# Gate products moved to GpSimd, the last two packs scored by halves, and 131 instead of 130 packs taken off ScalarE

## The chip, the cores and the metric

The kernel runs on one core of one Trainium2 chip. The metric is the device time of one launch in microseconds (us), as a median over runs; less is better. The engines are called PE (TensorE), ACT (ScalarE), DVE (VectorE), POOL (GpSimd) and SP (SyncE, which here only issues DMAs).

## The reference

There are 2048 tokens of width 512 and 32 heads of 16. Two attention branches read the same `x`; a gate per token mixes them. `x @ wqkv` and the final `@ wo` are there in both.

```python
g = sigmoid((x * gate_w).sum(-1, keepdims=True))
# branch A: softmax attention
scores = einsum("bhqd,bhkd->bhqk", q, k) * (Dh ** -0.5)
o = einsum("bhqk,bhkd->bhqd", softmax(scores), v)        # then @ wo
# branch B: linear attention, its features are two softmaxes over 16 numbers
phi_q = concat([softmax(pq), softmax(-pq)]); phi_k = ...  # pq = q @ w_phi
num = phi_q @ (phi_k^T v); den = phi_q . sum(phi_k)       # then num / den @ wo
out = g * a + (1 - g) * b
```

Branch A has 32 heads x 2048 x 2048 scores, and each wants an exponential. That is most of the work.

## The kernel before

**Units, packs, groups.** A unit is the scores of one head for 128 keys and 512 queries: one matmul with 32 rows of contraction, a tile of 128 x 512 in one bank of PSUM. Four units (four heads, same keys and queries) make a pack; 16 packs (all 2048 keys) make a group, whose sums stand in one PSUM bank; there are 32 groups, so 512 packs. Eight groups go over one chunk of 512 queries, so the run has four chunks.

**Two ways to the exponential.** Most packs go through ACT: `_qk` writes the scores of three or two units into a ring of five PSUM banks (`RING`), and `_exp` (line 1183) reads them in one activation of 1536 or 1024 columns, alternately, into the ring `ET` in SBUF; `_pv` then multiplies them with the values (line 1250). The scores of an activation are written while the activation before it runs. The packs in `self.spot` go another way: `_vector_bits` has DVE turn each score into the bits of a bfloat16 number (line 962, four instructions of 128 x 512 from PSUM for a pack), `_vector_terms` adds a shift to those bits in SBUF for two further terms, and the three terms are all multiplied with the values (12 matmuls for a pack). The first shift is done by DVE for up to two packs together (line 984, 2048 or 4096 columns), and so is the second but for the last of the three `SHIFTS`, which `_pool_term` gives to POOL in two pieces of 1024 columns (line 999). `AWAY` says with one bit mask for each group which packs are in `spot`: key tiles 1, 4, 7, 10 and 13 can be. Its masks have 130 bits set. By chunks of queries these are 29, 34, 32 and 35 packs.

**Normalizing.** When a group is summed, `_norm_a` and `_norm` turn it: DVE transposes the bank into `T1` (line 1271), and after each pair of groups POOL multiplies the sums with the gate (`n_den`, line 1278), DVE takes reciprocals (line 1280) and multiplies the attention values with them into `T2` (`n_mul`, line 1282; 15 of 128 x 512 and one of 128 x 256 for group 30). DMAs on SP's queue turn `T2` into `onTA`, from which the output projection `_out` (its helper `_quarters`, line 651) reads. The last group has a path of its own, `_norm_last` (lines 1105 to 1117), in two halves of 256 queries, all on DVE.

**The end.** `_last_pack` treats pack 511 by halves: all its scores are written, then ACT does the first 256 queries of the four units, then the other 256 (line 1070), and the first half is multiplied with its values and normalized while ACT does the second. The four output tiles of the last chunk follow: two leave PSUM by ACT (line 1619), two by DVE (line 1615), and DMAs store them (line 1624).

**The order.** `Plan.order` is a list scheduler. It gives every engine a fixed queue from costs, priorities and due times; on the chip each engine takes its queue in order and waits on semaphores. `SHIFT` moves the due times of single tasks by up to 14 packs. PE gets matmuls with zeros (line 1257) where it would have little to do. `PORT` and the variable `port` in `order` keep POOL's instructions and certain ones of DVE apart in the plan, and make POOL's wait for DVE's.

Of the kernel before, what the change touches and what calls it, by code (L numbers as in the profile page):

```python
# [389 lines left out]
class _Kernel:  # L390
# [364 lines left out]
    def _gate(self):  # L755
# [44 lines left out]
    AWAY = (26, 27, 26, 31, 22, 13, 15, 15, 31, 15, 13, 31, 30, 23, 31, 15, 29, 31, 26, 27, 31, 26, 31, 21, 31, 31, 28, 31, 31, 11, 23, 31)  # L800

    SHIFT = (
# [166 lines left out]
    def _vector_terms(self, turn, packs):  # L969
# [6 lines left out]
        for k, (shift, scaled) in enumerate(SHIFTS):  # L976
            if k == 2 or k == 1 and turn % self.EVERY == 0:
                for j, pack in enumerate(packs):
                    b = self.b_vp[k][j]
                    self._pool_term(pair, j, k, shift, b, packs[0] + self.TERM)  # L980
                    self.terms[pack].append((lambda k=k, j=j: self.vp[:, k, j], b, scaled))
# [688 lines left out]
```

## Time and profile before

| | |
|---|---|
| time, median of 3 runs | 737.9 us (737.86 to 738.07) |
| the profiled execution, its own time | 737.4 us |
| its span, first to last instruction | 735.6 us |
| ACT busy | 723.5 us, 98% |
| DVE busy | 690.5 us, 94% |
| PE busy, matmuls with zeros included | 713.1 us, 97% |
| POOL busy | 303.8 us, 41% |
| granted PE clock | 1.000 |

Busy time is the union of an engine's instructions. A duration in a row of instructions is longer than the step to the next one on the same engine, since the next starts before the last result is written; where steps matter they are taken from stretches of several instructions. The span is 1.8 us shorter than the time of its execution.

### The profile page before, as it was taken

To read this page: it belongs to the slowest core of one execution; us is meant where nothing else is said; L and a number is where in the kernel's file an instruction comes from. 1 tells how busy PE (TensorE), PEld (TensorE's weight loads), DVE (VectorE), ACT (ScalarE), POOL (GpSimd) and SP (SyncE) were. 2 spreads that over 40 slices of the span, in tenths; PEclk is the share of its full clock that TensorE was granted. 3 is DMA by queue.
4 is the path that set the end of the run, shared out by engine and by line. 5 is a ranking of instruction groups with operands and counts; after the bars stand their busy time and mean duration, and the time that the engine had idled before them with its cause. 6 is when DMAs were issued, how large, how long until landed. Compare 5 with 4: busy or idle time off the path is not lost.

```text
span 735.6 us, 19777 instructions
## 1 busy us (share of the span) xinstructions
PE 713.1 (97%) x8549; PEld 234.4 (32%) x8549; DVE 690.5 (94%) x1085; ACT 723.5 (98%) x636; POOL 303.8 (41%) x318
## 2 busy tenths in 40 slices
PE   8999999999999999999999999999999999999998
PEld 3334233243223223332232233333332233332322
DVE  4899999988999999999999999999999999999996
ACT  6999999999999999999999999999999999999996
POOL 3832342424544424535353344334334444344442
PEclk9999999999999999999999999999999999999999
DMA  9400100001010010100001032042123111003210
GB/s 201 145 10 6 22 2 9 16 4 18 4 15 11 4 20 2 17 11 8 14 2 17 15 61 28 8 83 35 23 45 74 21 16 23 16 25 63 40 29 30
DMA packets 90041, 21.96 MB, mean 30 GB/s; under 512 B 82913, under 2 KB 89441, under 8 KB 89953
## 3 DMA queue, kind: packets, MB, share of 16 engines
q1 hardware_dynamic: 88752, 20.30, 14.5%
q8 instruction: 67, 1.10, 0.7%
q10 hardware_dynamic: 1200, 0.39, 0.2%
q14 instruction: 22, 0.17, 0.1%
HBM read 4.21 MB, written 2.10 MB: 9 GB/s over the span
## 4 chain that ended last, share of the span: by engine, by line
ACT 73%; PE 13%; DVE 11%; DMA 1%; issue 0%; POOL 0%; DVEq 0%; POOLq 0%
ACT ET L1183 70%; PE ps L1131 5%; DVE va L962 4%; PE ps L1250 4%; ACT bq L1425 3%; PE ps L651 2%; DVE vp L984 2%; DVE btree L1414 1%; DMA xT<-in_A_x_dram 1%; PE ps L744 1%; PE ps L1257 1%; DVE bq L1423 0%; DVE VB L1541 0%; DVE nb L1541 0%; DVE rb L1539 0%
## 5 line engine op out<-in xcount | busy, mean ns | idle before, releaser
L1183 ACT ACTIVATE ET<-ps 128x1536 bf16<-128x1536 f32 (+1 forms) x612 | 692.9, 1343 | 4.6 <-PE ps L1131 4.4
L999 POOL TENSOR_SCALAR vp<-va 128x1024 uint16<-128x1024 uint16 x264 | 275.7, 1044 | 337.3 <-DVE vp L984 124.2
L962 DVE TENSOR_SCALAR va<-ps 128x512 uint16<-128x512 f32 x520 | 339.5, 681 | 23.9 <-PE ps L1131 21.7
L1131 PE MATMUL ps<-qT,kT 32*128 32x512 bf16 (+1 forms) x2053 | 311.0, 384 | 10.1 <-ACT ET L1183 5.1
L1131 PEld LDWEIGHTS ps<-qT,kT 32*128 32x128 bf16 x2053 | 82.7, 91 | 258.3 <-ACT ET L1183 146.5
L984 DVE TENSOR_SCALAR vp<-va 128x4096 uint16<-128x4096 uint16 (+1 forms) x151 | 162.0, 1079 | 0.6 <-PE ps L1250 0.2
L1250 PE MATMUL ps<-ET,V 128*32 128x512 bf16 x1532 | 149.0, 385 | 1.3 <-DVE T L1271 1.0
L1250 PE MATMUL ps<-vp,vc 128*32 128x512 bf16 x1040 | 93.9, 384 | 0.3 <-DVE vp L984 0.2
L1250 PEld LDWEIGHTS ps<-ET,V 128*32 128x32 bf16 x1532 | 39.3, 95 | 64.9 <-issue 48.6
L651 PE MATMUL ps<-WB,xT 128*32 128x512 bf16 x768 | 57.4, 382 | 0.5 <-DVE bq L1395 0.3
L1250 PE MATMUL ps<-va,V 128*32 128x512 bf16 x520 | 51.3, 385 | 0.0
L1250 PE MATMUL ps<-vp,V 128*32 128x512 bf16 x520 | 48.2, 383 | 0.3 <-DVE vp L984 0.2
L1257 PE MATMUL ps<-kT,zero 128*32 128x512 bf16 x468 | 42.1, 384 | 0.0
L651 PE MATMUL ps<-xT,WA 128*32 128x512 bf16 x480 | 36.1, 382 | 0.6 <-DVE va L962 0.4
L1250 PEld LDWEIGHTS ps<-vp,vc 128*32 128x32 bf16 x1040 | 24.7, 95 | 35.3 <-issue 20.2
L1425 ACT ACTIVATE bq<-bq 128x2048 bf16<-128x2048 bf16 x16 | 31.5, 1989 | 0.1
L1271 DVE STREAM_TRANSPOSE T<-ps 128x512 f32<-128x512 f32 x31 | 21.9, 708 | 1.1 <-PE ps L1250 1.0
L651 PE MATMUL ps<-WoB,WT 128*32 128x512 bf16 x256 | 22.6, 383 | 0.3 <-DVE va L962 0.3
L1395 DVE CAST bq<-ps 128x512 bf16<-128x512 f32 x32 | 21.7, 678 | 0.3 <-PE ps L651 0.2
L651 PEld LDWEIGHTS ps<-WB,xT 128*32 128x32 bf16 x768 | 15.2, 95 | 19.9 <-issue 10.4
L651 PE MATMUL ps<-WoA,onTA 128*32 128x512 bf16 x256 | 21.2, 381 | 0.0
L744 PE MATMUL ps<-WA,xT 128*128 128x128 bf16 x256 | 19.5, 220 | 0.7 <-DVE va L962 0.4
(94 smaller groups left out, 367.1 us busy)
## 6 DMA issues: line engine op xcount, KB each, us to landing
turned<-T SPq DMA_DIRECT2D x240, 8.0 KB, 1.8
qT<-qs SPq DMA_DIRECT2D x120, 16.0 KB, 1.8
WB<-in_B_wqkv_dram SPq DMA_DIRECT2D x1, 1536.0 KB, 6.9
out_dram<-WB SPq DMA_DIRECT2D x12, 128.0 KB, 2.0
WA<-in_A_wqkv_dram SPq DMA_DIRECT2D x3, 384.0 KB, 5.1
WoA<-in_A_wo_dram SPq DMA_DIRECT2D x1, 512.0 KB, 8.0
WoB<-in_B_wo_dram SPq DMA_DIRECT2D x1, 512.0 KB, 8.9
out_dram<-xT SPq DMA_DIRECT2D x3, 128.0 KB, 1.8
```

Of the source, the lines that this page charges most:

```text
L651: ins = e.matmul(out[32 * g:32 * g + 32], lhs[:, 32 * g:32 * g + 32], rhs, start=start, stop=stop, tile_position=(0, 32 * g), skip_group_c ...
L744: ins = e.matmul(self._bank(job)[:, P * tt:P * tt + P], self.xT[:, c, QCH * j + TOK * tt:QCH * j + TOK * tt + TOK], self.WA[:, 2, c, P * c ...
L962: parts.append(op("DVE", lambda e, j=j, job=job: e.tensor_scalar(self.va[:, pair, side, j, :], self._bank(job), SCALE * LOG2E * 128.0, (12 ...
L984: self.plan.op("DVE", lambda e, k=k, shift=shift: e.tensor_scalar(flat(self.vp[:, k]), flat(self.va[:, pair]), float(shift), None, op0=ALU ...
L999: o = self.plan.op("POOL", lambda e, flat=flat: e.tensor_scalar(flat[0], flat[1], 1.0, float(shift), op0=ALU.mult, op1=ALU.add), 0.08 + n ...
L1131: return e.matmul(out, self.kT[32 * i:32 * i + 32, cp, kt * TOK:(kt + 1) * TOK], self.qT[32 * i:32 * i + 32, s, at], start=True, stop=True ...
L1183: o = plan.op("ACT", lambda e: e.activation(self.ET[:, a % NS:a % NS + n, at], self.ps[:, self._ring(a):self._ring(a) + n, at], ACT.Exp, s ...
L1250: ins = e.matmul(self._bank(ot)[32 * i:32 * i + 32, at], V[:, v0:v0 + 32], tile(), start=(kt == 0), stop=(kt == self.NT - 1), tile_positio ...
L1257: ins = e.matmul(self._bank(ot)[32 * i:32 * i + 32, :], self.zero[:], self.kT[:, 0, 0:QCH], start=False, stop=False, tile_position=(0, 32 ...
L1271: self.turned_out = op("DVE", lambda e: e.transpose(T1[:, side].rearrange("p b s -> p (b s)"), src()), 0.635, deps=last, writes=[b_T1[side ...
L1395: [lambda e, b, k=k: e.tensor_copy(bq[:, k].rearrange("p (g s v) -> p g s v", g=8, s=2)[:, :, 0, :], b.rearrange("p (g v) -> p g v", g=8))],
L1425: op("ACT", lambda e, side=side: e.activation(sides[side], sides[side], ACT.Exp, scale=1.0 - 2 * side), self.c_act(2048) + 0.04, reads=[bu ...
```

## The change

Five things are changed:

1. `AWAY` has 131 bits set instead of 130; by chunks of queries 29, 34, 34 and 34 packs. Other packs of a group are chosen than before.
2. `SHIFT` is another list: of its 756 entries (778 before) six are as they were. So the order of all queues is another.
3. `n_mul` in `_norm` is issued to POOL instead of DVE.
4. Of the last pack in `spot`, the second piece of the last term is done by DVE instead of POOL.
5. `_last_pack` gives way to `_last_packs`: packs 510 and 511 are both taken by halves of the queries. The scores of one unit of pack 510 and one of pack 511, 256 queries each, share one PSUM bank. ACT does the first 256 queries of both packs in two activations of 1024 columns, then the second 256 in one of 1536 and one of 512. The value products of both packs come in two halves as well.

```diff
-    AWAY = (26, 27, 26, 31, 22, 13, 15, 15, 31, 15, 13, 31, 30, 23, 31, 15, 29, 31, 26, 27, 31, 26, 31, 21, 31, 31, 28, 31, 31, 11, 23, 31)
+    AWAY = (18, 31, 14, 27, 27, 26, 29, 27, 31, 15, 13, 31, 29, 15, 31, 27, 21, 31, 31, 15, 14, 23, 31, 31, 14, 31, 29, 31, 29, 27, 27, 31)
     SHIFT = (
...
-    def _pool_term(self, pair, j, k, shift, b, due):
+    def _pool_term(self, pair, j, k, shift, b, due, last):
...
+            if c and last:
+                o = self.plan.op("DVE", lambda e, flat=flat: e.tensor_scalar(
+                    flat[0], flat[1], float(shift), None, op0=ALU.add), 0.07 + n * QCH * 0.00026, reads=[src],
+                    deps=b.readers or b.writers, writes=[sink], name="v_term", prio=due)
+            else:
+                o = self.plan.op("POOL", ...
...
-        cut = len(self.mine) - 4
+        cut = len(self.mine) - 8
...
-        self._last_pack(cut)
+        self._last_packs(cut)
...
+    def _last_packs(self, cut):
...
+        for half in range(2):
+            at, a, of = self._columns(half), 0, {}
+            while a < 4:
+                b = a + 1
+                while b < 4 and self._ring(cut + 4 * half + b) not in (0, 3):
+                    b += 1
+                banks = [self._ring(cut + 4 * half + x) for x in range(a, b)]
+                mine = units[a:b] + units[4 + a:4 + b]
+                m, o = self._halves(mine, banks, cut % NS, a, at, users)
...
+            for p in range(units[0] // 4, self.NPACK):
...
+                o = plan.op("PE", lambda e, p=p, src=src, at=at: self._values(e, self.ot[g], g % 8, p % NT, src, at=at),
+                            0.12, name=f"pv{p}", prio=p + 2.5, kind="col", array=0.1066,
+                            deps=self.b_V[g % 8 // 2][p % NT // 4].writers + [self.pvs[units[0] // 4 - 1]]
+                            + [of[u] for u in range(4 * p, 4 * p + 4)] + ([self.turned_out] if half else []))
...
+            plan.of(f"g{g}", self._norm_last, g, half, done + ([] if half else self.late))
...
+    def _halves(self, units, banks, slot, first, at, users):
+        plan, n = self.plan, len(units)
+        ps = self.ps[:, banks[0]:banks[-1] + 1, :].rearrange("p r (h q) -> p r h q", h=2)
+        to = self.ET[:, slot:slot + 8, at].rearrange("p (k r) q -> p r k q", k=2)[:, first:first + n // 2]
+        def run(e):
+            for k, u in enumerate(units):
+                ins = self._scores(e, u, ps[:, k % (n // 2), k // (n // 2), :], at)
+            return ins
+        m = plan.op("PE", run, 0.23, ..., deps=self.qks[-1:] + [users[r] for r in banks])
...
+        o = plan.op("ACT", lambda e: e.activation(to, ps, ACT.Exp, scale=SCALE), self.c_act(QCH // 2 * n), deps=deps, ...
...
-        op("DVE", lambda e: e.tensor_tensor(
+        op("POOL", lambda e: e.tensor_tensor(
             T2[:].rearrange("p b (s d) -> p s b d", s=2)[:, lo:hi], T1[:, lo:hi, :, 0:16],
-            rinv[:, lo:hi, :, None].to_broadcast([P, n, 16, 16]), ALU.mult), 0.065 + 0.269 * n,
+            rinv[:, lo:hi, :, None].to_broadcast([P, n, 16, 16]), ALU.mult), 0.24 + 0.45 * n,
            reads=reads + [b_rinv], writes=[b_T2], name="n_mul", prio=due)
```

More of the change, by code (lines that the diff above doesn't have):

```diff
@@ L979, in _vector_terms @@
                     b = self.b_vp[k][j]
-                    self._pool_term(pair, j, k, shift, b, packs[0] + self.TERM)
+                    self._pool_term(pair, j, k, shift, b, packs[0] + self.TERM, pack == max(self.spot))
                     self.terms[pack].append((lambda k=k, j=j: self.vp[:, k, j], b, scaled))
@@ L998, in _pool_term @@
             src.writers = bits.writers[c:c + n]
-            o = self.plan.op("POOL", lambda e, flat=flat: e.tensor_scalar(
-                flat[0], flat[1], 1.0, float(shift), op0=ALU.mult, op1=ALU.add), 0.08 + n * QCH * 0.00102,
-                reads=[src], deps=b.readers or b.writers, writes=[sink], name="p_term", prio=due)
+            if c and last:
[3 more added lines that the diff above has]
+            else:
+                o = self.plan.op("POOL", lambda e, flat=flat: e.tensor_scalar(
+                    flat[0], flat[1], 1.0, float(shift), op0=ALU.mult, op1=ALU.add), 0.08 + n * QCH * 0.00102,
+                    reads=[src], deps=b.readers or b.writers, writes=[sink], name="p_term", prio=due)
             bits.readers.append(o)
@@ L1037, in _attention @@
                     self.plan.of(f"y{len(self.pvs)}", self._out, len(self.pvs) // (8 * NT) - 1)
-        self._last_pack(cut)
+        self._last_packs(cut)
         self.plan.of(f"y{len(self.pvs)}", self._out, NQC - 1)
-    def _last_pack(self, cut):
-        plan, NT, NS, p = self.plan, self.NT, self.NSLOT, self.NPACK - 1
-        wrap = cut + -cut % self.RING
-        parts = [(cut, wrap), (wrap, cut + 4)] if cut < wrap < cut + 4 else [(cut, cut + 4)]
-        users = {self._ring(x): self.exps[self.in_group[x]] for x in range(cut - self.RING, cut)}
-        scores = []
-        for a, b in parts:
-            units = self.mine[a:b]
-            def run(e, a=a, units=units):
-                for k, u in enumerate(units):
-                    ins = self._scores(e, u, self.ps[:, self._ring(a + k), :])
-                return ins
-            o = plan.op("PE", run, 0.23, reads=self._score_bufs(units), name=f"qk{len(self.qks)}", prio=-1000, kind="row",
-                        array=0.0533 * (b - a), deps=self.qks[-1:] + [users[self._ring(x)] for x in range(a, b)])
-            o.commit = "now", (units[-1] + 1) // 4
-            o.tiles = [u % 4 for u in units]
-            o.slack = max(0.0, self.exps[-1].cost - self.AHEAD)
-            self.qks.append(o)
-            scores.append(o)
-        g, kt = divmod(p, NT)
-        g8, ot, done = g % 8, self.ot[g], [self.pvs[p - 1]]
-        for hook in self.hooks.get(p, ()):
-            hook()
-        values = []
-        for half in range(2):
-            at, exps = self._columns(half), []
-            for (a, b), m in zip(parts, scores):
-                o = plan.op("ACT", lambda e, a=a, b=b, at=at: e.activation(
-                    self.ET[:, a % NS:a % NS + b - a, at], self.ps[:, self._ring(a):self._ring(a) + b - a, at], ACT.Exp,
-                    scale=SCALE), self.c_act(QCH // 2 * (b - a)),
-                    deps=[m] + [self.pvs[self.mine[x - NS] // 4] for x in (a, b - 1)],
-                    name=f"exp{len(self.exps)}", prio=p + 1)
-                if half:
-                    o.commit = "banks", [self._ring(x) for x in range(a, b)]
-                self.exps.append(o)
-                exps.append(o)
-            src = {u % 4: lambda slot=self.place[u] % NS, at=at: self.ET[:, slot, at] for u in range(4 * p, 4 * p + 4)}
-            plan.tag = f"p{p}"
-            o = plan.op("PE", lambda e, src=src, at=at: self._values(e, ot, g8, kt, src, at=at), 0.12, name=f"pv{p}",
-                        prio=p + 2.5, kind="col", array=0.1066, deps=self.b_V[g8 // 2][kt // 4].writers + done + exps)
-            plan.tag = None
-            o.tiles = list(src)
-            if not half:
-                o.commit = "close", None
-                plan.of(f"g{g}", self._norm_last, g, half, [o] + self.late)
-                done = [o, self.turned_out]
-            else:
-                plan.of(f"g{g}", self._norm_last, g, half, [o])
-        self.pvs.append(o)
-        self.late = []
@@ new lines, in _last_packs @@
+    def _last_packs(self, cut):
+        plan, NT, NS, RING = self.plan, self.NT, self.NSLOT, self.RING
+        users = {}
+        for x in range(cut - RING, cut):
+            users[self._ring(x)] = self.exps[self.in_group[x]]
+        units, packs, left = self.mine[cut:], [], {0: [], 1: []}
+        closing = self.NPACK - 1
+        assert cut % NS <= NS - 8
+        g = closing // NT
+        for half in range(2):
+            at, a, of = self._columns(half), 0, {}
[6 more added lines that the diff above has]
+                m, o = self._halves(mine, banks, cut % NS, a, at, users)
+                if 4 * half + b > 3:
+                    o.commit = "banks", [r for x, r in zip(range(a, b), banks) if 4 * half + x > 2]
+                for r in banks:
+                    users[r] = o
+                for u in mine:
+                    of[u] = o
+                a = b
+            done = []
+            for p in range(units[0] // 4, self.NPACK):
+                if p in self.spot:
+                    if not half:
+                        self._pv(p)
+                    continue
+                if not half:
+                    for hook in self.hooks.get(p, ()):
+                        hook()
+                src = {u % 4: lambda slot=self.place[u] % NS, at=at: self.ET[:, slot, at] for u in range(4 * p, 4 * p + 4)}
+                plan.tag = f"p{p}"
+                o = plan.op("PE", lambda e, p=p, src=src, at=at: self._values(e, self.ot[g], g % 8, p % NT, src, at=at),
+                            0.12, name=f"pv{p}", prio=p + 2.5, kind="col", array=0.1066,
+                            deps=self.b_V[g % 8 // 2][p % NT // 4].writers + [self.pvs[units[0] // 4 - 1]]
+                            + [of[u] for u in range(4 * p, 4 * p + 4)] + ([self.turned_out] if half else []))
+                plan.tag = None
+                o.tiles = [2, 3] if p == closing else [0, 1]
+                if not half and p == closing:
+                    o.commit = "close", None
+                done.append(o)
+                if not half:
+                    self.pvs.append(o)
+            plan.of(f"g{g}", self._norm_last, g, half, done + ([] if half else self.late))
+        self.pvs[-1] = done[-1]
+        self.late = []
@@ new lines, in _halves @@
+    def _halves(self, units, banks, slot, first, at, users):
[6 more added lines that the diff above has]
+            return ins
+        m = plan.op("PE", run, 0.23, reads=self._score_bufs(units), name=f"qk{len(self.qks)}", prio=-1000, kind="row",
+                    array=0.0267 * n, deps=self.qks[-1:] + [users[r] for r in banks])
+        m.commit = "now", (units[-1] + 1) // 4
+        m.tiles = [u % 4 for u in units[:(n + 1) // 2]]
+        m.slack = max(0.0, self.exps[-1].cost - self.AHEAD)
+        self.qks.append(m)
+        deps = [m]
+        if at.start == 0:
+            for u in (units[0], units[-1]):
+                x = self.place[u] - self.NSLOT
+                deps.append(self.pvs[self.mine[x] // 4])
+        o = plan.op("ACT", lambda e: e.activation(to, ps, ACT.Exp, scale=SCALE),
+                    self.c_act(QCH // 2 * n), deps=deps, name=f"exp{len(self.exps)}", prio=units[0] // 4 + 1)
+        self.exps.append(o)
+        return m, o
```

205 rows, old and new, of the table SHIFT are left out of this document.

## The prediction

> **What bounds the kernel now.** I read the page's busy times first, then the waits of ACT, then the chain of work, then DVE's load by stretches, and last the timeline of the end.
>
> ```profile
> PE 713.1 (97%) x8549; PEld 234.4 (32%) x8549; DVE 690.5 (94%) x1085; ACT 723.5 (98%) x636; POOL 303.8 (41%) x318
> ...
> ACT 73%; PE 13%; DVE 11%; DMA 1%; issue 0%; POOL 0%; DVEq 0%; POOLq 0%
> ```
> ```profile
> ACT ET L1183 <- PE ps L1131: 4.4, 1, 4.4
> ACT xT L1619 <- PE ps L651: 2.9, 1, 2.9
> ACT L1183 <- issue: 1.8, 1, 1.8
> ```
>
> The first line ranks the engines; the chain is ACT for 73%. The three lines of waits (us in total, times, longest) are all that ACT ever waited: once before its first activation, once after its last one, and once at launch. So ACT is full from its first exponential to its last, and inside that stretch only less work on ACT can shorten the run. ACT's work is priced by stretches of the chain in which it runs alone:
>
> ```profile
> 69.45 40.78 ACT ET L1183 x36
> ...
> 676.48 49.84 ACT ET L1183 x44
> ```
>
> The activations alternate between three units and two, so 36 of them hold 90 units: 40.78 / 90 = 0.453 us for a unit of 128 x 512 scores; 44 hold 110, 49.84 / 110 = 0.453 again. A pack of four units is 1.81 us.
>
> **131 packs.** One pack more in `spot` takes 4 x 0.453 = 1.81 us from ACT, and with ACT full that is path. What it puts on DVE, and what else changes there:
>
> ```profile
> 470.31 1.20 DVE va L962 x2
> ...
> 481.69 0.60 DVE T L1282
> ...
> 489.12 1.14 DVE vp L984
> ...
> 491.46 0.60 DVE vp L984
> ```
>
> These are steps of DVE when it goes from one instruction to the next: 0.60 for the bits of a unit, 0.60 for a gate product of 512 columns, 1.14 for a term of two packs, 0.60 for that of one. Four more bits: +2.4. The masks make 57 pairs and 17 single packs instead of 54 and 22; each has two terms on DVE, but the first pair only one. So 113 terms of two packs instead of 107 and 34 of one instead of 44: 6 x 1.14 - 10 x 0.60 = +0.8. The piece of the last term that comes over from POOL has half the columns of a single: at most +0.6, taken as 0.4. Gate products: 15 x 0.60 leave, and the one of 256 columns, about 0.4: -9.4. In sum DVE has 5.8 us less, 684.7. PE gets twelve value matmuls for four, and some twenty more of half width at the end:
>
> ```profile
> L1250 PE MATMUL ps<-vp,vc 128*32 128x512 bf16 x1040 | 93.9, 384 | 0.3 <-DVE vp L984 0.2
> ...
> L1257 PE MATMUL ps<-kT,zero 128*32 128x512 bf16 x468 | 42.1, 384 | 0.0
> ```
>
> At 93.9 / 1040 = 0.09 us, 8 more cost 0.7 us and twenty halves about 1. The cover is the second row: 42.1 us of matmuls with zeros, which the plan sets only where PE has room. Taken at nothing; 1.7 us if that cover were not there when wanted.
>
> **The gate products on POOL.** No row shows this product on POOL. The nearest:
>
> ```profile
> L1493 POOL TENSOR_TENSOR kvbd<-kvacc,bm 128x256 bf16<-128x256 f32 x2 | 1.2, 616 | 0.4 <-DVE kvbd L1497 0.3
> L1448 POOL TENSOR_TENSOR bsum<-bsum,VB 128x128 f32<-128x128 f32 x4 | 2.1, 518 | 0.7 <-DVE VB L1447 0.5
> ```
>
> From 128 to 256 columns it grows by 98 ns, which gives 616 + 196 = 0.81 us for 512; doubling 616 gives 1.23. I take 1.0, nearer to the row with the same types (bfloat16 from float32). 15 x 1.0, 0.6 for the short one and one more term piece are 17 us on an engine that is busy for 303.8 of 735.6: no bound. What is new is that SP's queue waits for POOL before it issues the 16 DMAs of each pair of groups, and behind these in the queue stand the DMAs of the next queries, the transposes of branch B and the stores.
>
> ```profile
> POOL vp L999 <- DVE vp L984: 124.2, 68, 9.1
> ...
> 715.54 0.41 DVE L1282 TENSOR_TENSOR T<-T,rinv 128x256 bf16<-128x256 f32 x1
> ...
> 730.05 0.40 DVE L1117 STREAM_TRANSPOSE onTA<-T 128x256 bf16<-128x256 bf16 x1
> ```
>
> POOL waits up to 9.1 us for DVE before a term, so a product could come about that much later than now. The tightest place is the end: group 30's product at 715.54 must be done before the back transpose at 730.05, 14 us on. I take nothing for the delay; without that cover it would cost up to the 9.1 us, once.
>
> **The end.** The rows of the last 9 us:
>
> ```profile
> 726.66 2.10 ACT L1070 ACTIVATE ET<-ps 128x256 bf16<-128x256 f32 x4
> ...
> 728.11 0.39 PE L1250 MATMUL ps<-vp,vc 128*32 128x512 bf16 x4
> ...
> 728.55 0.45 DVE L1105 STREAM_TRANSPOSE T<-ps 128x256 f32<-128x256 f32 x1 [1.72 <-PE ps L1250]
> ...
> 729.05 0.10 PEld L1250 LDWEIGHTS ps<-ET,V 128*32 128x32 bf16 x4 [0.19 <-DVE T L1105]
> ...
> 729.47 0.29 DVE L1113 TENSOR_TENSOR T<-T,rinv 128x128 bf16<-128x128 f32 x1
> 729.68 0.44 DVE L1105 STREAM_TRANSPOSE T<-ps 128x256 f32<-128x256 f32 x1
> ...
> 731.10 0.45 DVE L1117 STREAM_TRANSPOSE onTA<-T 128x256 bf16<-128x256 bf16 x1
> 731.46 1.27 DVE L1615 TENSOR_TENSOR xT<-xT,ps 128x512 bf16<-128x512 f32 x2
> ...
> 732.14 1.31 SPq L1624 DMA_DIRECT2D out_dram<-xT  x3
> ```
>
> The last exponential ends at 726.66 + 2.10 = 728.76, and the span ends 6.84 us later. The second half's values start at 729.05 because the first half's transpose had to leave the bank; then the steps of both halves are interleaved on DVE, and the second half's back transpose ends at 731.55, 2.79 after the last exponential. After the change the second half is 2048 columns of ACT, some 1.85 us, instead of 1.05, so the first half is out of the way 0.8 us sooner. The second half's values can start 0.14 after the last exponential instead of 0.29, but are eight matmuls instead of four (+0.1), so its transpose still starts about 0.9 after it. Behind that it has DVE for itself: in the first half, transpose to end of product took from 728.55 to 729.76, 1.2 us, and a back transpose makes it 1.65; 0.9 + 1.65 = 2.55 instead of 2.79. DVE's two outputs and SP's three stores, back to back above, lose one member each to an earlier time: another 0.1 to 0.2. Sum 0.4; bounds 0 (the store's landing hides it) and 0.8 (the whole head start).
>
> ACT's own last instructions: now four short ones take 2.10 for four units, which at the long-run pace are 1.81. After it four take eight units, 3.62 at that pace, with fewer instructions per column. 0 to 0.2 less, taken as 0.1. The new wait here is that the scores of the activation of 1536 need the bank of the one of 1024 two before it, and have only another of 1024 to run under, behind which ACT, and the values, would stand. That is how each activation of 1536 runs already, with no wait in the list above: taken at 0, at most 0.2.
>
> **The sum**: 1.8 + 0.1 + 0.4 = 2.3 off the profiled execution's 737.4 (span 735.6): 735.1, span 733.3. The median of the runs shown is 737.9, 0.5 above that execution; so 735.6, or 0.31% less. Bounds of the known terms: 1.8 + 0.2 + 0.8 gives 735.1, 1.8 - 0.2 gives 736.3. A measurement of this kernel can tell about 0.2% from no change, 1.5 us: below 736.4 is faster, above 739.4 slower.
>
> **Rivals.** *DVE runs out in the third chunk of queries (slower).* The masks put 34 packs instead of 32 there.
>
> ```profile
> 368.00:552.00 184.00, 180.33 (x2164) 57.38 (x2160) 178.27 (x289) 183.91 (x160) 76.48 (x78) 1.00 0.18 32
> 552.00:729.00 177.00, 172.95 (x2066) 54.65 (x2062) 169.00 (x268) 176.75 (x158) 77.56 (x79) 1.00 0.18 32
> ```
> ```profile
> DVE va L962 <- PE ps L1131: 3.9, 11, 0.7
> ```
> ```profile
> 650.00:700.00 50.00, 48.70 (x566) 15.38 (x562) 49.30 (x82) 49.98 (x46) 22.48 (x24) 1.00 0.24 42
> ```
>
> The first two rows are the third and the last chunk (span, then busy PE, PEld, DVE, ACT, POOL). DVE idles 5.7 us in the third. Two packs add 2 x (4 x 0.60 + 1.14) = 7.1, four gate products take 2.4 away, and ACT goes through it 8 x 0.453 = 3.6 faster: 5.7 - 7.1 + 2.4 - 3.6 = -2.6. DVE would have 2.6 us too much to do, and 6.5 if the 3.9 us it waited for PE there (second fence) stay. ACT then stands still for 2.6 to 6.5 us, 735.6 becomes 738.2 to 742.1, middle 740.1. It decides from 3.8 us on that can't be moved. Against it: the last chunk has 8.0 us idle before and gets one pack less, so branch B's tasks and the bits of later packs, which are due 8 to 16 packs (some 20 us) ahead, can move over the border; and in the last fence DVE was busy for 49.30 of 50 us with ACT at 49.98. Chance 0.16.
>
> *The products hold DVE up.*
>
> ```profile
> 719.65 1.22 DVE L984 TENSOR_SCALAR vp<-va 128x4096 uint16<-128x4096 uint16 x1
> ...
> 720.96 1.04 POOL L999 TENSOR_SCALAR vp<-va 128x1024 uint16<-128x1024 uint16 x1 [1.16 <-DVE vp L984]
> ...
> 721.39 1.69 DVE L984 TENSOR_SCALAR vp<-va 128x4096 uint16<-128x4096 uint16 x1
> ```
>
> A term of 4096 columns takes 1.22 us alone, but 1.69 when it starts at 721.39 inside a POOL instruction that ends at 722.00. If every product blocked DVE for its whole 1.0 us, the third chunk would lack another 4.0 us, 6.6 to 10.5 in all: 742.2 to 746.1. Against it: 162.0 us of terms beside 264 such pieces are stretched little in this trace, and the plan keeps the two apart. Chance 0.04. The Trainium skill has this as an exclusive lock (SBUF — State Buffer, "Who interferes with whom"): a DVE instruction in a two-port mode, or with two SBUF inputs against a reading GpSimd one, blocks fully against GpSimd, whoever starts second; the trace agrees, 0.47 us for a remaining 0.61. By the GPSIMD Engine Reference, "Engine selection", two-input work is about twice as slow there, which would make an estimate of 1.4 us a product; no run yet shows it.
>
> *The saving is eaten by waits.* The present order keeps ACT without a single wait for 721 us, and the new one is another order throughout. Waits of 0.5 to 2.2 us in all, or an end that gains nothing besides, would leave 736.1 to 737.8, as if the change didn't do what it says. Nothing in the profile of before shows the new order; for it speaks that the span of ACT has no slack at all, against it that DVE gets 5.8 us less work. Chance 0.18.
>
> **Numbers.** Forecast 0.62, eaten 0.18, third chunk 0.16, products 0.04. Faster by over 0.2% (under 736.4): the forecast and 0.04 of the eaten case, 0.66. Slower by over 0.2% (over 739.4): 0.12 of the third chunk and the products, 0.16. The rest, 0.18, is the same. The range begins at 734.9, a little under the lower bound, and reaches 738.9, which leaves out most of the two slow cases and little else.
>
> **What the changed profile would show.** Right: ACT's list of waits as short as before; the last exponential 1.9 us earlier, about 726.9; the second half's back transpose ending 2.5 us after it; products on POOL of 0.8 to 1.2 us; DVE's busy time about 685. Wrong: many short waits of ACT for scores (the order), or waits gathered in 368 to 550 with DVE over 99% busy there (the third chunk), or terms and branch B's instructions of DVE stretched beside the products (the lock). A last exponential at the old time would mean that the pack's saving was lost; an end of 6.8 us after it, that the halves gave nothing.

## The result, and the profile after

| | before | after |
|---|---|---|
| time, median of 11 runs each | 737.85 us (737.71 to 738.13) | 735.96 us (735.79 to 736.57) |
| ratio, 95% interval | | 0.9976 (0.9967 to 0.9985) |
| profiled execution: its own time, span | 737.4, 735.6 | 736.27, 734.5 |

The change saves 1.9 us, 0.24%; 2.3 were forecast. The page after, busy times and chain by engine, and ACT's list of waits (us in total, times, longest):

```profile
PE 712.3 (97%) x8547; PEld 233.8 (32%) x8547; DVE 687.2 (94%) x1070; ACT 721.4 (98%) x633; POOL 319.1 (43%) x335
...
ACT 70%; PE 23%; DVE 6%; DMA 1%; issue 0%; DVEq 0%
```
```profile
ACT ET L1210 <- PE ps L1158: 5.0, 2, 4.8
ACT xT L1646 <- PE ps L651: 3.3, 1, 3.3
ACT L1210 <- issue: 1.7, 1, 1.7
```

ACT is as full as it was: apart from 0.2 us in all it waits only before its first activation and behind its last. The two profiled executions lie 1.1 us apart and not 1.9, mostly because the second one starts later, which is outside the change. These are the first activations in the timelines of before and of after:

```profile
7.42 0.81 ACT L1183 ACTIVATE ET<-ps 128x768 bf16<-128x768 f32 x1 [4.38 <-PE ps L1131]
```
```profile
7.86 0.81 ACT L1210 ACTIVATE ET<-ps 128x768 bf16<-128x768 f32 x1 [4.83 <-PE ps L1158]
```

The start waits for the first transposes of `x` from DRAM and moved between 7.2 and 8.3 us over the profiles of this study, kernels with the same start among them. The timeline of the last 11 us after the change:

```profile
723.56 3.89 ACT L1116 ACTIVATE ET<-ps 128x1024 bf16<-128x1024 f32 x4
...
725.75 0.69 DVE L981 TENSOR_SCALAR vp<-va 128x2048 uint16<-128x2048 uint16 x1 [0.70 <-PE ps L1277]
726.06 0.11 PEld L1158 LDWEIGHTS ps<-qT,kT 32*128 32x128 bf16 x2 [0.42 <-ACT ET L1116]
...
726.38 0.62 PE L1277 MATMUL ps<-vp,vc 128*32 128x512 bf16 x8
...
726.82 0.39 PE L1277 MATMUL ps<-ET,V 128*32 128x256 bf16 x8
...
727.27 0.45 DVE L1132 STREAM_TRANSPOSE T<-ps 128x256 f32<-128x256 f32 x1 [0.82 <-PE ps L1277]
...
727.83 0.18 PEld L1277 LDWEIGHTS ps<-ET,V 128*32 128x32 bf16 x8 [0.25 <-issue]
...
729.81 0.45 DVE L1144 STREAM_TRANSPOSE onTA<-T 128x256 bf16<-128x256 bf16 x1
```

The last exponential ends at 723.56 + 3.89 = 727.45. So the span divides into: start 7.42 to 7.86 (+0.44), first to last exponential 728.76 - 7.42 = 721.34 to 727.45 - 7.86 = 719.59 (-1.75), and the end 735.6 - 728.76 = 6.84 to 734.5 - 727.45 = 7.05 (+0.2). The gain lies in ACT's stretch alone. The new end brought nothing behind it.

### The profile page after: what moved, and what is told of

Its sections match the earlier page's. It is cut to its first block, busy times and chain, and to the rows that moved or that the text cites. A ratio compares the mean times of both kernels' runs of the same rounds, so it can differ in the third digit from the quotient of the medians.

```text
span 734.5 us, 19764 instructions
## 1 busy us (share of the span) xinstructions
PE 712.3 (97%) x8547; PEld 233.8 (32%) x8547; DVE 687.2 (94%) x1070; ACT 721.4 (98%) x633; POOL 319.1 (43%) x335
## 4 chain that ended last, share of the span: by engine, by line
ACT 70%; PE 23%; DVE 6%; DMA 1%; issue 0%; DVEq 0%
ACT ET L1210 67%; PE ps L1158 8%; PE ps L1277 7%; PE ps L651 4%; ACT bq L1452 3%; DVE va L959 3%; PE ps L744 1%; DMA xT<-in_A_x_dram 1%; PE ps L1284 1%; DVE vp L981 1%; DVE btree L1441 0%; DVE bq L1450 0%; DVE kT L691 0%; DVE WB L1399 0%; PE ps L1183 0%; PE ps L1394 0%
## 5 line engine op out<-in xcount | busy, mean ns | idle before, releaser
L981 DVE TENSOR_SCALAR vp<-va 128x4096 uint16<-128x4096 uint16 (+1 forms) x147 | 163.9, 1122 | 1.5 <-PE ps L1277 0.9
L1284 PE MATMUL ps<-kT,zero 128*32 128x512 bf16 x444 | 40.6, 385 | 0.0
L1309 POOL TENSOR_TENSOR T<-T,rinv 128x512 bf16<-128x512 f32 (+1 forms) x16 | 16.5, 1031 | 17.1 <-DVE rinv L1307 7.3
```

The costliest lines, as they stand in the source:

```text
L981: self.plan.op("DVE", lambda e, k=k, shift=shift: e.tensor_scalar(flat(self.vp[:, k]), flat(self.va[:, pair]), float(shift), None, op0=ALU ...
L1284: ins = e.matmul(self._bank(ot)[32 * i:32 * i + 32, :], self.zero[:], self.kT[:, 0, 0:QCH], start=False, stop=False, tile_position=(0, 32 ...
L1309: op("POOL", lambda e: e.tensor_tensor(T2[:].rearrange("p b (s d) -> p s b d", s=2)[:, lo:hi], T1[:, lo:hi, :, 0:16], rinv[:, lo:hi, :, No ...
```

## The experiments

Twelve kernels ran, four to a chip, each beside the kernel before. Five or three rounds were timed, one for the two with an empty `SHIFT`.

**1. The products put back on DVE, order kept.** In `build`, after the order is made:

```diff
             p.order()
+            q = p.queues
+            for o in [o for o in q["POOL"] if o.name == "n_mul"]:
+                q["POOL"].remove(o)
+                q["DVE"].insert(max(q["DVE"].index(d) for d in o.deps if d.eng == "DVE") + 1, o)
+                o.eng = "DVE"
```

> The changed kernel with its order kept instruction for instruction, only the 16 gate products are put back from POOL's queue into DVE's, each right behind the last DVE instruction that it needs. Theory A (ACT is the bound, DVE has room): DVE gets about 15 x 0.6 = 9 us more, ACT's waits grow by at most 0.3 us in all, 735.9 to 736.3 against 737.85 for the kernel before. Rival D (DVE needed the relief for the 131st pack): DVE idles 4.6 us in 368 to 552 us now, four products take 2.4 of that, and ACT starts to wait for scores behind it: 737 to 740.

Measured: 748.36 us (before 737.78), ratio 1.0123 (1.0101 to 1.0146). Two of its six runs took 743.8; the granted PE clock was 1.000 in these and 0.993 in the four at 748.4, of which the profile is one. ACT's first wait there, and its busy times by windows (span, PE, PEld, DVE, ACT, POOL, then the clock):

```profile
ACT ET L1215 <- PE ps L1163: 13.7, 15, 5.0
```
```profile
475.00:480.00 5.00, 4.29 (x55) 1.23 (x47) 4.97 (x9) 5.00 (x5) 0.27 (x1) 1.00 0.10 32
480.00:484.00 4.00, 3.83 (x29) 0.84 (x29) 2.77 (x6) 2.64 (x4) 1.58 (x2) 0.65 0.05 15
484.00:488.00 4.00, 4.00 (x32) 0.80 (x28) 3.02 (x5) 2.29 (x2) 2.18 (x4) 0.50 0.01 4
488.00:492.00 4.00, 4.00 (x39) 0.94 (x37) 3.88 (x4) 2.85 (x3) 0.45 (x1) 0.57 0.00 0
```

Theory A falls: some 9 us on an engine that is busy for 94% cost 7.8 us even at full clock (743.8 against 735.96), more than rival D's 737 to 740 as well. Of the 13.7 us in the line above, 5.0 are ACT's wait for the start, which every run has. The other 14 waits, 8.7 us, are new, and ACT's busy time grew by 3.2 us (724.6 instead of 721.4) with the same number of activations, from starts too little late to show as waits (see the last section). How a product gets to ACT, at one of them:

```profile
612.58 1.38 DVE L1314 TENSOR_TENSOR T<-T,rinv 128x512 bf16<-128x512 f32 x1
...
613.88 1.87 DVE L964 TENSOR_SCALAR va<-ps 128x512 uint16<-128x512 f32 x3
...
614.62 0.60 PE L1163 MATMUL ps<-qT,kT 32*128 32x512 bf16 x4 [1.34 <-DVE va L964]
...
615.27 1.45 ACT L1215 ACTIVATE ET<-ps 128x1536 bf16<-128x1536 f32 x1 [1.02 <-PE ps L1163]
```

The product stands ahead of the bits of three units, and a term of POOL that runs from 612.38 to 613.42 holds it up besides (1.38 us; the products take 0.69 alone). DVE empties the bank late, PE waits 1.34 us for it, the scores for ACT stand behind on PE's queue, and ACT waits 1.02 us. In the changed kernel the same bits follow the reciprocal at once. A place further back in DVE's queue might have cost less; none was tried.

In the profiled run PE also thinned out after 475 us, its clock went to 0.65 and 0.50 of full speed until 492, and ACT starved meanwhile: 4.2 of its waits lie between 475 and 500 us.

**2. Only the products moved, in the kernel before, order kept.** The same surgery the other way, by planned start time:

```diff
             p.order()
+            q = p.queues
+            for o in [o for o in q["DVE"] if o.name == "n_mul" and o.cost > 0.25]:
+                q["DVE"].remove(o)
+                q["POOL"].insert(sum(x.start < o.start for x in q["POOL"]), o)
+                o.eng = "POOL"
```

> The kernel before with its order kept, only the 16 gate products are moved from DVE's queue to POOL's, at the place where the plan had them in time. Theory A: nothing changes, 737.6 to 738.1, since ACT is as full as it was; DVE's busy time falls by 9. Rival D: DVE's relief shortens late starts of ACT, 0.3 to 1 us less, 736.9 to 737.5. Lock rival: the products hold DVE's terms up, 0.3 to 1 us more.

Measured: 738.27 against 737.78, ratio 1.0007 (0.9999 to 1.0016). The page's busy times:

```profile
PE 709.7 (96%) x8534; PEld 234.5 (32%) x8549; DVE 685.5 (93%) x1069; ACT 723.8 (98%) x636; POOL 324.1 (44%) x334
```

DVE's busy time falls by 5.0 us (690.5 to 685.5; 9 were expected) and nothing is gained. Much of the missing 4 us shows in the timelines of POOL and DVE, of which these are the worst pair:

```profile
565.82 1.06 POOL L1287 TENSOR_TENSOR T<-T,rinv 128x512 bf16<-128x512 f32 x1
```
```profile
565.85 2.10 DVE L989 TENSOR_SCALAR vp<-va 128x4096 uint16<-128x4096 uint16 x1
```

Put into POOL's queue by time alone, the products got into DVE's way. Five DVE instructions beside a product took 3.3 us longer in all than they do alone (this term 2.10 instead of 1.22), and three products took about 2.0 us instead of 1.06. So this is half of the relief, and 738.27 lies in the lock rival's range, just above theory A's. What it shows is that 5 us less on DVE give nothing in an order that keeps ACT full. That the whole 9 would give nothing either isn't shown; for it speaks that ACT has no wait there to lose. In the changed order the products on DVE cost 7.8 us and more (experiment 1).

**3. The old end in the changed kernel.** `_last_pack` of before in the place of `_last_packs`, `cut` 4 units from the end.

```diff
-        cut = len(self.mine) - 8
+        cut = len(self.mine) - 4
-        self._last_packs(cut)
+        self._last_pack(cut)
```

> The changed kernel with the old end (the last pack alone by halves, as before); the order is the same up to the last 12 us. Prediction's step: the new end is worth 0.4 to 0.5, so this is 736.3 to 736.5. Theory L (the first half is held by the late terms of the last pack in spot, not by ACT, so its head start is lost): the same as the changed kernel within 0.2, 735.8 to 736.2.

Measured: 736.60, ratio 0.9986 (0.9977 to 0.9995), so about 0.6 more than the changed kernel's 0.9976, though the intervals overlap. That is the size of the prediction's step, but it isn't the head start that is lost. The last line of ACT's waits, and the timeline at that place:

```profile
ACT ET L1072 <- PE ps L1133: 0.5, 1, 0.5
```
```profile
726.00 1.94 ACT L1072 ACTIVATE ET<-ps 128x1024 bf16<-128x1024 f32 x2 [0.53 <-PE ps L1133]
```

In this order the old end makes ACT wait 0.53 us for the last pack's scores, which it doesn't in the kernel before.

**4. The terms of packs 503 and 506 earlier.**

```diff
-("t503", 13)
+("t503", 0)
```

> The changed kernel with one entry of SHIFT set from 13 to 0, that of the terms of packs 503 and 506; DVE then does their second term before the terms of pack 509 instead of between them, and PE's last 10 us follow; nothing else moves. Theory L: the values of the last pack's terms come earlier, the first half's transpose starts 0.4 to 0.8 us sooner than its 0.18 us before the last exponential's end, the second half has DVE for itself, and the end is 0.2 to 0.4 shorter: 735.5 to 735.8. Prediction's step as it stood (ACT alone times the halves): no change, 735.9 to 736.1.

Measured: 735.84, ratio 0.9975 (0.9967 to 0.9984): no change. Timeline:

```profile
722.89 3.90 ACT L1116 ACTIVATE ET<-ps 128x1024 bf16<-128x1024 f32 x4
...
724.31 0.68 DVE L981 TENSOR_SCALAR vp<-va 128x2048 uint16<-128x2048 uint16 x1
...
725.40 0.39 PE L1158 MATMUL ps<-qT,kT 32*128 32x256 bf16 x2
...
725.95 0.60 PE L1277 MATMUL ps<-vp,vc 128*32 128x512 bf16 x8
...
726.38 0.39 PE L1277 MATMUL ps<-ET,V 128*32 128x256 bf16 x8
...
726.83 0.45 DVE L1132 STREAM_TRANSPOSE T<-ps 128x256 f32<-128x256 f32 x1 [1.83 <-PE ps L1277]
```

Pack 509's last term is ready at 724.99 instead of 726.44, yet the first half's transpose still starts with the last exponential's end (726.83 and 722.89 + 3.90 = 726.79). So it was not DVE that held it. PE's queue has the last scores first, which wait for ACT until 725.40, then the terms of pack 509, then the first half's values. Theory L, as I had put it, falls; what the rows show is the queue.

**5. Those terms ahead of the last scores on PE.** Besides the edit of 4:

```diff
             p.order()
+            pe = p.queues["PE"]
+            last = [o for o in pe if o.name == "pvx"][-3:]
+            for o in last:
+                pe.remove(o)
+            at = max(k for k, o in enumerate(pe) if o.name.startswith("qk"))
+            pe[at:at] = last
```

> The changed kernel, the entry of SHIFT for packs 503 and 506 set to 0 (as in the run before), and on PE's queue the three groups of matmuls for the terms of pack 509 moved ahead of the last scores; nothing else moves. Theory Q (PE's queue holds the first half: the terms of pack 509 stand between the last scores and the first half's values): the values of the first half come right behind the last scores, its transpose starts 0.6 to 0.8 us earlier, about 0.7 us before the last exponential's end, the second half has DVE for itself, and the end is 6.75 to 6.9 us after the last exponential instead of 7.05 to 7.1: 735.5 to 735.7. Rival (the end hangs on output matmuls and stores, not on the halves): the transpose moves, the time stays at 735.8 to 736.0.

Measured: 735.99, ratio 0.9977 (0.9967 to 0.9986): no change. Timeline (span 734.08):

```profile
726.26 0.39 PE L1164 MATMUL ps<-qT,kT 32*128 32x256 bf16 x2
...
726.68 0.60 ACT L1122 ACTIVATE ET<-ps 128x512 bf16<-128x512 f32 x1 [0.17 <-PE ps L1164]
727.03 0.45 DVE L1138 STREAM_TRANSPOSE T<-ps 128x256 f32<-128x256 f32 x1 [1.83 <-PE ps L1283]
```

The transpose now leads the last exponential's end (726.68 + 0.60 = 727.28) by 0.25 us, less than the 0.7 that theory Q expected, but the end is 734.08 - 727.28 = 6.80 us, 0.25 to 0.3 shorter, as it said. The price is on ACT. The last scores come at 726.26, 3.16 us after the first of the last four activations (723.10); in experiment 4 it was 725.40 - 722.89 = 2.51. So the last activation starts late, with 0.17 us of it shown as a wait, and ACT's stretch is 727.28 - 7.26 = 720.02 us instead of 719.59. What the end gains ACT loses: in this order PE has time for one of the two. The time lies in the rival's range, but not for the rival's reason, since the end did get shorter.

**6. The products twice on DVE, in the kernel before, order kept.**

```diff
             p.order()
+            q = p.queues["DVE"]
+            for o in [o for o in q if o.name == "n_mul" and o.cost > 0.25]:
+                x = Op("DVE", o.fn, o.cost, "n_again", o.prio, -99, "full", o.lat)
+                for u in p.ops:
+                    u.deps = [x if d is o else d for d in u.deps]
+                x.deps = [o]
+                q.insert(q.index(o) + 1, x)
```

> The kernel before with its order kept, only each of the 16 gate products is done twice on DVE, the second time right behind the first; the result is the same. This adds to DVE of the kernel before what the changed one lost when its products were put back. Theory T (DVE has no room at those places in either order; the 131st pack has nothing to do with it): it costs like there, 4 to 8 us, 742 to 746. Rival D (it is the 131st pack that filled DVE): the kernel before has room for 9 us more on DVE, 737.8 to 739.

Measured: 747.84 against 738.01, ratio 1.0132 (1.0118 to 1.0146). ACT's first wait:

```profile
ACT ET L1190 <- PE ps L1138: 9.0, 14, 4.2
```

4.2 of these 9.0 us are the wait for the start, and here too ACT's busy time grew, by 3.5 us (727.0 instead of 723.5). With 130 packs and an idle 45 us on DVE, 9 us more on DVE cost 9.8, above both expectations. So experiment 1 doesn't say that the 131st pack had filled DVE. Either order breaks where its instructions are delayed.

**7. The products on DVE, order made anew.** `op("POOL"` back to `op("DVE"` for `n_mul`, with its old cost; `AWAY` and `SHIFT` of after.

> The changed kernel with the gate products on DVE, and the order made anew by its scheduler with that cost, same AWAY and SHIFT. Theory T (a fixed order can't take new work, a new order can, at the price of an order that nobody chose): 737 to 741, below the 743.8 of the kept order. Rival D (131 packs and the products are more than DVE can do in any order): as slow as the kept order, 743 to 748.

Measured: 795.34, ratio 1.0779 (1.0740 to 1.0817), outside both expectations. The first of ACT's waits:

```profile
ACT ET L1210 <- PE ps L1158: 20.8, 22, 4.6
```

**8. Only the 131st pack, in the kernel before.**

```diff
-    AWAY = (..., 31, 31, 11, 23, 31)
+    AWAY = (..., 31, 31, 15, 23, 31)
```

> The kernel before with one bit more in its mask (pack 474, group 29), so 131 packs, products on DVE, old end; same SHIFT, and the order is new only from about 455 packs on. Theory A (ACT is the bound and DVE has 8 us of room in the last chunk): 1.8 us less, 735.8 to 736.3. Rival D (a further pack fits only where DVE was relieved): ACT waits, 737 to 741.

The bit that is set is that of pack 471 (29 x 16 + 7), not 474. Measured: 745.25, ratio 1.0099 (1.0085 to 1.0113), above both expectations. One place in the timeline makes most of it:

```profile
676.62 4.35 DVE L962 TENSOR_SCALAR va<-ps 128x512 uint16<-128x512 f32 x7
...
680.89 0.71 DVE L1271 STREAM_TRANSPOSE T<-ps 128x512 f32<-128x512 f32 x1
...
681.65 0.62 PE L1250 MATMUL ps<-ET,V 128*32 128x512 bf16 x4 [1.43 <-DVE T L1271]
...
682.32 1.02 ACT L1183 ACTIVATE ET<-ps 128x1024 bf16<-128x1024 f32 x1 [5.49 <-PE ps L1250]
```

DVE does seven units' bits in a row; the group's transpose stands behind them; PE's next values need the bank that it empties, and ACT waits for these values, not for scores. The wait is 5.49 us, three times what the pack takes off ACT.

**9. The pack and the products together, in the kernel before.** The edits of 8 and 2.

> The kernel before with the one pack more (pack 474, as in the run with the pack alone, 745.25) and its gate products moved to POOL's queue at the same places in time. Theory T (the loss there is one bad spot of an order that nobody chose, where value matmuls stand ahead of scores): products on POOL can't mend the 5.5 us wait, 743 to 745.5. Rival D (DVE had no room for the pack without the relief): most of the 7.3 us comes back, 736 to 739.

Measured: 746.84, ratio 1.0127 (1.0113 to 1.0140), above both expectations, so the products on POOL bring nothing of the loss back. The wait stays:

```profile
ACT ET L1188 <- PE ps L1255: 5.5, 1, 5.5
```

**10 and 11. `SHIFT = ()`**, in the changed kernel and in the one before.

> The changed kernel with an empty SHIFT: same packs, products on POOL, same end, the order as the scheduler makes it from the unmoved due times. Theory T (what keeps ACT full is the chosen order, not the products on POOL): many waits of ACT as in the run with the order made anew, 770 to 810. Rival D (the products on DVE made that run slow): 737 to 750.

> The kernel before with an empty SHIFT. Theory T: as slow as the changed kernel with an empty SHIFT, within some 15 us either way, since the list is what differs most from order to order: 760 to 810. Rival D: the changed parts are worth several us by themselves, so this is slower than the other by 5 or more, or with room left on DVE at 740 to 750.

Measured: 791.97, ratio 1.0734 (1.0708 to 1.0760), and 800.71, ratio 1.0853 (1.0833 to 1.0872). The first of ACT's waits in the first of them:

```profile
ACT ET L1108 <- PE ps L1175: 40.6, 17, 12.4
```

Without its list the changed kernel is 56 us slower, with products on POOL and the new end; so the 795 of experiment 7 isn't the price of products on DVE, but of an order to which the list doesn't belong. The changed one is 8.7 us ahead of the other here; that is one order of each, and whether the parts or chance did it stays open.

**12. Only the new end, in the kernel before.** `_last_packs` and `_halves` of after, `cut` 8 units from the end.

> The kernel before with only the new end (packs 510 and 511 both by halves); the order is the same up to the last 12 us. Prediction's step: the end is worth 0.4 to 0.5, 737.3 to 737.5. Theory W (the 0.6 that the old end costs in the changed kernel is one wait of ACT, 0.53 us at 726.0, that the old end does not have in the order of before; the first half's head start is eaten by PE's queue): nothing, 737.7 to 738.1.

Measured: 738.08 against 738.00, ratio 1.0000 (0.9991 to 1.0009). Nothing, as theory W said. The timeline (span 737.32):

```profile
726.47 3.78 ACT L1114 ACTIVATE ET<-ps 128x1536 bf16<-128x1536 f32 x4
...
730.27 0.45 DVE L1130 STREAM_TRANSPOSE T<-ps 128x256 f32<-128x256 f32 x1 [1.82 <-PE ps L1275]
```

The first half's transpose again begins only with the last exponential's end (730.25), and the end is 7.07 us, 0.2 longer than the old end's 6.84, as in the changed kernel. This execution is the slowest of the eleven (739.12); ACT has two waits more in it, 0.62 us at 32.9 and 0.44 at 513.1, far ahead of the end.

## Why the prediction was right, and where it wasn't

**The bound and the pack: right.** 735.6 us was forecast and 735.96 came. ACT stayed full, and its stretch is 1.75 us shorter, where 1.8 for the pack and 0.1 for fewer short instructions were counted. (The last exponential was to come at 726.9 and came at 727.45, 1.3 us earlier than before and not 1.9, because the start came 0.44 later.)

**The end: wrong size.** The term of 0.4 failed at the step "so the first half is out of the way 0.8 us sooner". In the kernel before, the first half's transpose led the last exponential's end by 0.21 us (728.55 and 728.76), after the change by 0.18 (727.27 and 727.45). ACT had twice as much to do behind the first half as before, but PE took the first half's values only after the last scores and the last pack's terms (experiments 4 and 5), and when these were put first ACT paid. The rest of the term fell with it: the second half's values were to start 0.14 us after the last exponential and started 0.38 after it (727.83; 0.29 before), and its back transpose ended at 730.26, 2.81 us after it, where 2.55 was counted and 2.79 stood before. The end came out at 7.05 us, past the 6.8 that the prediction named as the sign that the halves gave nothing. By itself the new end is worth nothing (experiment 12); in the changed order it avoids a wait of 0.53 us (experiment 3). With 0 instead of 0.4 the sum is 1.9 off the 737.9 of the runs shown, 736.0, and 735.96 came.

**The products on POOL: right, with one surprise.** The rows of POOL and of DVE's terms:

```profile
L1309 POOL TENSOR_TENSOR T<-T,rinv 128x512 bf16<-128x512 f32 x15 | 15.9, 1058 | 14.2 <-DVE rinv L1307 7.3 <-DVE btree L1457 2.8 <-DVE bq L1450 2.1
```
```profile
L981 DVE TENSOR_SCALAR vp<-va 128x4096 uint16<-128x4096 uint16 x113 | 140.5, 1251 | 0.6 <-PE ps L1277 0.2
```

1.06 us each where 1.0 was taken, and not the 1.4 of the estimate beside it; not on the path. DVE came to 687.2 instead of 684.7: its terms of 4096 columns take 1251 ns on average instead of 1237, 1.6 us over 113, which is the lock (see below); the other 0.9 isn't traced to a cause. The surprise is how much hangs on their place: left on DVE in this order they cost 7.8 us (experiment 1), while in the order of before the 5 us that came off DVE were worth nothing (experiment 2).

**The rival of the third chunk: didn't happen.** Third and last chunk (span, PE, PEld, DVE, ACT, POOL):

```profile
368.00:552.00 184.00, 180.55 (x2125) 56.33 (x2117) 179.43 (x283) 183.85 (x161) 79.61 (x82) 1.00 0.16 30
552.00:727.00 175.00, 171.21 (x2077) 54.74 (x2079) 167.77 (x266) 175.00 (x155) 78.60 (x82) 1.00 0.19 35
```

DVE idles 4.6 us in the third, where the sum had 2.6 too little, and 7.2 in the last, where 8.0 before, a pack (3.5) and products (2.2) less and 1.8 of ACT more would make 15.5. So about 7 us of work lie on the other side of the border, as the point against that rival had it. (The border itself comes 3.6 us sooner after the change, at 548.4; counted from there DVE idles 4.5 and 7.3 us.) Counted by shape, it is branch B: of its 128x1024 tree steps on DVE (`btree<-bq`) six fell into the third chunk and two into the last, and now four into each.

**The lock: real, and rare for the products.** Two of the 15 products held a term up; one, in the timelines of POOL and DVE:

```profile
297.09 1.06 POOL L1309 TENSOR_TENSOR T<-T,rinv 128x512 bf16<-128x512 f32 x1
```
```profile
297.80 1.43 DVE L981 TENSOR_SCALAR vp<-va 128x4096 uint16<-128x4096 uint16 x1
```

The term took 1.43 us instead of 1.22, 0.21 more, from an overlap of 297.80 to 298.15. Of the terms of 4096 columns that stand singly in the timeline (89 of 113, and 94 of 107 in the kernel before) 14 were made longer by an instruction of POOL that was still running, 12 of them by others than products, and 6 in the kernel before. In all 20 the term took longer than 1.22 us by what was left of POOL's instruction less 0.13 to 0.15 us, as 0.21 for 0.35 here, and an overlap of up to 0.14 us cost nothing. The pair of experiment 2 lost 0.88 for 1.03. The other way round it holds too: in experiment 1 a product on DVE that met a term of POOL lost 0.69 us for 0.84. The rule of the Trainium skill (SBUF — State Buffer, "Who interferes with whom"), that the one that comes second is blocked until the first is done, agrees but for these 0.14 us. The 14 lost 3.75 us together, the 6 before 1.95. So the products themselves cost DVE 0.4 us in the order delivered, where the plan keeps the two engines apart, and 3.3 where they were put by time alone (experiment 2).

**Eaten by waits: the rival that was nearest.** In the order delivered, ACT's new waits come to 0.2 us. But experiments 6 to 11 show how much the list carries: one more pack in an order that wasn't chosen for it cost 7.2 us, and no list 56. I gave the new order no price because nothing in the profile showed it, so that this term came out at nothing was not worked out, and to that extent the hit was luck. The order is what the other parts stand on. Whether an order with 131 packs exists without the products on POOL wasn't tried; it would take a search for the list.

## What to carry to other kernels

Where one engine is full and two others are over 90% busy in fixed queues, an average of 6% idle time is no room: 9 us put on DVE cost 8 to 12 us here, and 5 us taken off it gave nothing. Price an edit to such a kernel only together with the order that it will run in, and cost a head start by every queue that it must pass, here PE's, rather than by the engine that hands it over.

## What the runs showed of the hardware

**PE's clock fell without PE ever standing idle for long.** In experiment 1 PE was busy for 4.29 of the 5 us before its granted clock went to 0.65 and 0.50, and its longest idle stretch in them was 0.52 us. The four executions with this dip took 748.4 us, the two without it 743.8. By the Trainium skill (TensorE: Matmul & The Clock Gate, "Part 1: The HAM clock gate") the clock halves after an idle window of about 3.4 us. The halving agrees with the 0.50; an idle stretch of that length did not come before the dip.

**A list of waits doesn't show short late starts of ACT.** Two rows of the changed kernel's timeline, with no idle time before the second:

```profile
179.58 2.62 ACT L1210 ACTIVATE ET<-ps 128x1536 bf16<-128x1536 f32 x2
```
```profile
182.03 1.51 ACT L1210 ACTIVATE ET<-ps 128x1536 bf16<-128x1536 f32 x1
```
```profile
181.59 0.39 PE L1158 MATMUL ps<-qT,kT 32*128 32x512 bf16 x4
```

The last scores ahead of the second row were done at 181.98 (third row), 0.05 us before it. The pair of 1536 and 1024 columns took 182.03 - 179.58 = 2.45 us, where 40.78 / 18 = 2.27 is the mean of a pair. The groups by shape say why it counts as no wait:

```profile
L1210 ACT ACTIVATE ET<-ps 128x1536 bf16<-128x1536 f32 x302 | 471.7, 1562 | 0.5 <-PE ps L1158 0.2
L1210 ACT ACTIVATE ET<-ps 128x1024 bf16<-128x1024 f32 x302 | 344.9, 1142 | 0.0
```

The two last 1.56 + 1.14 = 2.70 us, so each runs on for about 0.2 us into the next one's time, and a start that is late by less than that leaves no gap. In experiments 1 and 6 it was ACT's busy time that grew by it, by 3.2 and 3.5 us.
